# A fused attention and feed-forward kernel on one core: two waits of the last batch's loads exchanged, and two feed-forward tiles of the first stage moved behind scores

## The chip, the cores and the metric

The kernel runs on 1 core of one Trainium2 chip. The metric is the device time of one execution in microseconds (us), as the median of several runs. Engines are named as in the profile: PE (TensorE, matrix products), DVE (VectorE), ACT (ScalarE), POOL (GpSimd), and SP, whose queue issues transfers. POOL also issues transfers, and writes their descriptors itself.

## The reference

Four batches of attention with 8 heads, 768 positions and head size 64 are followed by a feed-forward layer. Each query sees the keys within 15 positions and one summary per block of 32 positions (the maximum of the keys, the mean of the values).

```python
k_sum = k.reshape(B, H, nb, block, D).max(axis=3)
v_sum = v.reshape(B, H, nb, block, D).mean(axis=3)
scores_l = scale * q @ k^T, kept where |i - j| < window, else -1e9
scores_s = scale * einsum('bhsd,bhnd->bhsn', q, k_sum) + log(block)
a = softmax(concat([scores_l, scores_s]))
attn = a @ concat([v, v_sum])
x = attn as [B*S, H*D]                    # 3072 tokens, 512 wide
h = x @ w_in                              # 512 -> 2048
out = (h * sigmoid(1.702 * h)) @ w_out    # 2048 -> 512
```

Inputs and output are float32; the kernel works in bf16 and f16 between them.

## The kernel before, in words

The work is software-pipelined over the four batches: while PE does the feed-forward layer of one batch, the attention of the next is done beside it. A batch's 768 tokens are two halves of 384. The order on each engine is the order in which the program is written: every call goes through `_Ordered`, which keeps it, so an instruction that waits holds up all that stands behind it on its engine. Pools of buffers (`pmm`, four PSUM banks for matmul results; `psb`, two double banks for scores and turned tiles; `outp`, three output tiles `osb`) add waits where a buffer is still in use.

**Batch 0, the lead and the first input stage.** The first half's attention is done by functions of its own up to line 1029. Then the loop of line 1109 does the first feed-forward product of the first half: `ff_in` computes one tile of 128 of the 2048 columns as four matmuls (`ph`) and a GELU activation on ACT into `gT`. There are 16 tiles; two were done earlier (`N0` is 2). `q_late` turns the second half's queries of one head pair with six PE transposes (`ps_q`) and copies them into qT on DVE. The queries of the second half are loaded by POOL into `qb`, head pairs 0 to 3 apart (`load_q1`), between loads of w_in and w_out. Behind the tiles come the scores of the second half (`scores`, one call per head pair, 24 small matmuls `ps_s` and an exponential on ACT), the masks on DVE, the values (`ps_av`) and the turned x (`ps_x`), each put between parts of the first half's output product (`ff_out`, `po`, four matmuls a part) by the table `plan0`. `exp_soon` and `gelu_soon` make ACT load its exponential or GELU table ahead of use.

**Batches 1 to 3.** `load_batch(b)` issues on POOL the four loads of a batch's keys (`kb`, tag kb, two buffers) and the four of its queries (`qb`, two buffers). Transposing transfers on SP turn them: `xk` writes kx from `kb`, `xq` writes qT from `qb`. The values' rows are loaded straight into `vw` (`load_v`), and SP copies parts of them within SBUF (`halo_dmas`). `value_rows` also forms block sums of the values on PE (`ps_vs`), DVE adds them into `vs` (`block_sums`), and SP copies `vs` into `vw` as the sum rows (`sum_dmas`). For batch 3, `load_batch` copies one column to a tile `gate2` on POOL twice, which makes POOL's queue wait there: once for `vs`, once for the turned queries in qT.

In the loop of line 1154 with b = 1, PE does batch 1's feed-forward products: first the input tiles (16 for each half), then the output in seven products for each of three token tiles (`product`, with PSUM tiles poA, poB and poC). The output is put together by DVE in `osb` tiles and stored by SP. Beside it runs batch 2's attention; its result x is turned by transposing transfers on SP (`dx`, into xT). `load_batch(3)` is called after the second product, so that its waits and loads stand on POOL's queue at that place. The loop with b = 2 does the same for batch 2 beside batch 3's attention, with no further batch to load.

Of the kernel before, what the change touches and what calls it, by code (L numbers as in the profile page):

```python
# [9 lines left out]
F32 = mybir.dt.float32  # L10
# [25 lines left out]
def kernel(  # L36
# [10 lines left out]
    B, H, S, D = q.shape  # L47
# [5 lines left out]
    NP = H // 2  # L53
# [5 lines left out]
    NT = d_ff // 128  # L59
    HALF = S // 2  # L60
# [4 lines left out]
    dve = _Ordered(tc, nc.vector)  # L65
    act = _Ordered(tc, nc.scalar)
    pool = _Ordered(tc, nc.gpsimd)
# [55 lines left out]
    def load_turned(x, b, t2, name, gs_=(0, 1)):  # L123

        for g in gs_:
            t2[g] = castp2.tile([128, 2, NJ, 2, D], BF16, name=name, tag=name)
            for hh in range(2):
                h0 = hh * NP + 2 * g
                pool.dma_start(out=t2[g][:, :, :, hh].rearrange("p i a d -> p (i a) d"),
                               in_=x[b, h0:h0 + 2].rearrange("h (a p) d -> p (h a) d", p=128))  # L130

    def load_v(b):
        w5 = vw[b % 2].rearrange("p (j e) h c -> p j e h c", e=2)
        src = v[b].rearrange("h (j e p) d -> e j p h d", e=2, p=64)
        for j in range(NJ):
            for e in range(2):
                pool.dma_start(out=w5[e * 64:e * 64 + 64, j, e, :, 0:D], in_=src[e, j])
# [72 lines left out]
    qTs = [keep.tile([128, NP, S], BF16, name=f"qT{s}") for s in range(2)]  # L210
    qT = [[qTs[s][:, p] for s in range(2)] for p in range(NP)]
    vw = [keep.tile([128, NQ, H, VC], BF16, name=f"vw{s}") for s in range(2)]
    vs = keep.tile([128, H, VC], BF16, name="vs")
# [18 lines left out]
    def clear_values(eng, s):  # L232
        eng.memset(vw[s][96:128, 0], 0.0)
        eng.memset(vw[s][96:128, 0, :, D:VC], 1.0)
        eng.memset(vw[s][32:64, NQ - 1], 0.0)
        eng.memset(vw[s][32:64, NQ - 1, :, D:VC], 1.0)
# [8 lines left out]

    def load_batch(b):
        if b == 3:
            pool.tensor_copy(out=gate2[0:32], in_=vs[0:32, H - 1, 0:1])
        load_turned(k, b, kb2, "kb")
        if b == 3:  # L250
            pool.tensor_copy(out=gate2, in_=qTs[0][:, NP - 1, 0:1])
        load_turned(q, b, qb2, "qb", (0,) if b == 1 else (0, 1))
        if b == 2:
            load_v(b)

    def load_rest1():
        dve.memset(vw[1][:, :, :, D:VC], 1.0)
        clear_values(dve, 1)
        load_v(1)
        load_turned(q, 1, qb2, "qb", (1,))  # L260
# [12 lines left out]
    def copy(eng, out, in_):  # L273
        if eng is act:
            act.activation(out=out, in_=in_, func=ACT.Copy)
        elif eng == "dve_alone":

            dve.tensor_reduce(out=out, in_=in_.unsqueeze(len(in_.shape)), axis=AX.X, op=ALU.max)
        else:
            eng.tensor_copy(out=out, in_=in_)  # L280
# [91 lines left out]
    def turn_plain(ps, src):  # L372

        n, rows = src.shape[0], src.shape[2]
        for r in range(rows):
            for h in range(2):
                pe.transpose(out=ps[h * 64:h * 64 + 64, r * n:r * n + n], in_=src[:, h, r],
                             identity=ident[0:n, 0:n])
# [37 lines left out]
    def q_late(p, eng):  # L416
        if p < 2:
            ps = psb.tile([128, 2048], BF16, name="ps_q", tag="big")
        else:
            ps = pmm.tile([128, 1024], BF16, name="ps_q", tag="mm")  # L420
        turn_plain(ps[:, 0:HALF], qb2["late"][:, 2 * p:2 * p + 2])
        copy(eng, qT[p][0][:, HALF:S].rearrange("p (c r) -> p c r", r=JH),
             ps[:, 0:HALF].rearrange("p (r c) -> p c r", r=JH))
# [164 lines left out]
    def scores(b, half, p):  # L588
        a = a_sb[half, p] = attp.tile([128, 2, TH, QT], BF16, name="a_sb", tag="a_sb")
        big = psb.tile([128, 1024], F32, name="ps_s", tag="big")  # L590
        score_tiles(big, p, b % 2, half)
        act.activation(out=a.rearrange("p h t c -> p h (t c)"),
                       in_=big.rearrange("p (h c) -> p h c", h=2)[:, :, 0:HALF],
                       func=ACT.Exp, scale=scale)

    def mask(half, p):
        a = a_sb[half, p]
        dve.tensor_mul(a, a, mk[:, half * TH:(half + 1) * TH, :].unsqueeze(1)
                       .to_broadcast([128, 2, TH, QT]))

    def values(b, half, g, mm=False, between=()):

        if mm:
            banks = [pmm.tile([128, 512], F32, name="ps_av", tag="mm") for i in range(2)]
        else:
            ps = psb.tile([128, 1024], F32, name="ps_av", tag="big")
            banks = [ps[:, i * 512:i * 512 + 512] for i in range(2)]
        pvs = []
        for i in range(2):
            p = 2 * g + i  # L610
            a = a_sb[half, p]
            pv = banks[i][:, 0:390].rearrange("p (h j c) -> p h j c", h=2, j=JH)
            pvs.append(pv)
            for hh in range(2):
                for j in range(JH):
                    for e in range(2):
                        t = 2 * j + e
                        pe.matmul(out=pv[e * 64:e * 64 + 64, hh, j, :], lhsT=a[:, hh, t, :],
                                  rhs=vw[b % 2][:, half * TH + t, p + hh * NP if b else 2 * p + hh, 0:D + 1],
                                  start=True, stop=True, skip_group_check=True)  # L620
        x2[g] = attp.tile([128, 2, JH, 2, D], F16, name="x2", tag="x2", bufs=4)
        for i in range(2):
            norm(x2[g][:, :, :, i].rearrange("p h j d -> p j h d") if b else x2[g][:, i], pvs[i])
            if i == 0:
                for p in between:
                    mask(half, p)

    def norm(x, pv):
        rc = attp.tile([128, 2, JH, 1], F32, name="rc", tag="rc")
        dve.reciprocal(out=rc, in_=pv[..., D:D + 1])  # L630
        dve.tensor_mul(x.rearrange("p j h d -> p h j d"), pv[..., 0:D],
                       rc.to_broadcast([128, 2, JH, D]))
# [13 lines left out]
    def gelu(half, nt, ph):  # L646
        act.activation(out=gT[half][:, nt, :], in_=ph, func=ACT.Gelu_apprx_sigmoid)
# [3 lines left out]
    def ff_step(ph, half, nt, steps=range(KO)):  # L651
        for n in steps:
            g, i = n // 2, n % 2
            ko = g + 2 * i if halves[0] else 2 * g + i
            pe.matmul(out=ph, lhsT=w_in_sb[:, ko, nt * 128:(nt + 1) * 128],
                      rhs=xTT[half][g][:, i], start=(n == 0), stop=(n == KO - 1))
# [217 lines left out]
    N0 = 2  # L874
# [30 lines left out]
    gate2 = consts.tile([128, 1], BF16, name="gate2")  # L905
# [3 lines left out]
    def gelu_soon():  # L909

        act.activation(out=gate[:, 1:2], in_=gate[:, 0:1], func=ACT.Gelu_apprx_sigmoid)
# [120 lines left out]
    pmm = mid.enter_context(tc.tile_pool(name="pmm", bufs=4, space=bass.MemoryType.PSUM))  # L1032
# [5 lines left out]
    for e in range(2):  # L1038
        r = slice(64 * e, 64 * e + 64)
        dve.tensor_copy(out=w50[r, JH - e:NJ, e, :, 0:D],  # L1040
                        in_=v0n[r, :, JH - e:NJ, 0:D].rearrange("p h j d -> p j h d"))
# [4 lines left out]
    for p in range(NP):  # L1046
        k_late(p, dve)
        key_halos(p, 0, dve, JH)
        key_rows(p, 0, ks0[:, p, 0:nb], dve, JH)
    load_batch(1)  # L1050


    plan0 = {-1: ["s0", "s1"], 0: ["q2"], 1: ["m0", "q3", "m1", "s2", "s3"], 2: ["v0"],
             3: ["v1"], 4: ["x0"]}

    plan1 = {1: ["R"], 2: ["s00", "s01"], 4: ["t2", "t3", "m00", "m01"], 5: ["s10", "s11"],
# [7 lines left out]
    def beside0(slot):  # L1064
        for what in plan0.get(slot, ()):
            i = int(what[1])
            if what[0] == "q":
                q_late(i, dve)
            elif what[0] == "s":
                scores(0, 1, i)  # L1070
                if i == NP - 1:
                    gelu_soon()
            elif what[0] == "m":
                mask(1, i)
            elif what[0] == "v":
                values(0, 1, i, i == 0, (2, 3) if i == 0 else ())
            else:
                tx(1, i, act)

# [26 lines left out]
        sum_dmas(w5, 0)  # L1106


    for nt in range(N0, NT):
        ff_in(0, (nt,))  # L1110
        if nt == 14:
            for p in range(2):
                q_late(p, dve)
    early.close()
# [2 lines left out]
    ws = keep.tile([128, 4, NT // 2, N1], F16, name="ws")  # L1117
    exp_soon()
    beside0(-1)
    load_rest1()  # L1120
    for i, (ms, part) in enumerate((ms, part) for part in range(3) for ms in range(2)):
        ff_out(0, ms, part)
        beside0(i)
    for what, part in ((0, 0), (0, 1), (1, 0), (1, 1), (2, 0), (2, 1), (3, 0), (3, 1)):
        w_sum(what, part)

# [27 lines left out]
    for b in range(1, B - 1):  # L1154
# [34 lines left out]
        i = 0  # L1189
# [101 lines left out]
```

## Time and profile before

| what | value |
|---|---|
| runs | 207.1, 209.39 and 209.02 us; median 209.02 |
| profiled execution, its own time | 208.57 us |
| its span, first to last instruction | 206.6 us |
| PE busy | 196.6 us, 95% of the span |
| DVE busy | 145.3 us, 70% |
| ACT busy | 130.0 us, 63% |
| POOL busy | 91.3 us, 44% |
| loads by POOL's queue | 13.24 MB, 69648 packets |
| transfers by SP's queue | 14.39 MB, 26176 packets |

The profile shows one execution. A row of a timeline gives the start from the beginning of the span, the length, the engine, the line of the program (28 for all instructions, since a helper there records them), the operation with its output and inputs, how many were merged, and in brackets the time for which the engine stood idle before, with what ended it. A landing time is counted from a transfer's issue. In the row of slices the span is cut into 40 parts, and each digit is the busy share of a part in tenths.

### The profile page before, as it was taken

The numbers are of one execution on the slowest core, as the hardware profiler recorded it, in microseconds if no ns is written. First come the engines' busy times: TensorE is split into PE (matmuls) and PEld (weight loads), VectorE is DVE, ScalarE is ACT, GpSimd is POOL, SyncE is SP. The second block draws the span as 40 slices with busy tenths as digits, with TensorE's granted clock in tenths as the row PEclk, the third lists the DMA queues.
The fourth block names the chain that finished last, engine by engine and source line by source line (L and its number), as shares of the span: only waits on it lengthen the run. The fifth ranks groups of instructions, "written<-read, shape, count | busy, mean of one in ns | idle before, by whom it ended". The sixth has DMA issues, their size and how long they took to land.

```text
span 206.6 us, 5962 instructions
## 1 busy us (share of the span) xinstructions
PE 196.6 (95%) x2406; PEld 141.8 (69%) x2406; DVE 145.3 (70%) x397; ACT 130.0 (63%) x250; POOL 91.3 (44%) x141
## 2 busy tenths in 40 slices
PE   6999999999999999999999868999999999999993
PEld 6667654466787876566888744556888865568883
DVE  6676875968787764996769376797867666767221
ACT  4674869378776858778670526778771549985220
POOL 7964589358999521330691006900000008990000
PEclk9999999999999999999999999999999999999999
DMA  6999999999949999997499999999552740000223
GB/s 177 178 170 206 202 224 210 171 153 200 137 67 167 208 185 158 168 135 75 71 174 185 165 159 153 202 138 88 92 155 40 190 132 0 0 0 5 102 105 102
DMA packets 95995, 28.14 MB, mean 136 GB/s; under 512 B 83664, under 2 KB 93152, under 8 KB 95968
## 3 DMA queue, kind: packets, MB, share of 16 engines
q0 software_dynamic: 69648, 13.24, 84.2%
q1 hardware_dynamic: 26176, 14.39, 35.8%
q8 instruction: 19, 0.31, 0.6%
q10 hardware_dynamic: 144, 0.13, 0.2%
q14 instruction: 8, 0.07, 0.1%
HBM read 27.26 MB, written 6.29 MB: 162 GB/s over the span
## 4 chain that ended last, share of the span: by engine, by line
PE 86%; DMA 5%; DVE 4%; ACT 2%; issue 0%; DVEq 0%
PE ph L28 30%; PE poA L28 19%; PE poB L28 9%; PE poC L28 5%; PE phA L28 4%; PE ps_av L28 4%; DMA xT<-x 4%; PE ps_s L28 3%; PE po L28 2%; DVE ks L28 2%; DMA gT<-in_k_dram 2%; PE ps_t L28 1%; PE ps_x L28 1%; DVE qT L28 1%; PE phC L28 1%; PE phB L28 1%
## 5 line engine op out<-in xcount | busy, mean ns | idle before, releaser
L28 PE MATMUL ph<-xT,w_in_sb 128*128 128x384 f16 x400 | 68.1, 326 | 0.9 <-DMA xT<-x 0.8
L28 PEld LDWEIGHTS <-w_in_sb 128*128 128x128 f16 x442 | 42.6, 98 | 28.6 <-issue 1.5
L28 ACT ACTIVATE gT<-ph 128x384 f16<-128x384 f32 x100 | 47.7, 492 | 16.4 <-PE ph L28 15.7
L28 PEld LDWEIGHTS <-gs 128*128 128x128 f16 x352 | 33.5, 98 | 4.3
L28 POOL DMA_DIRECT2D vw<-in_v_dram x36 | 24.6, 700 | 22.2 <-DMA qb<-in_q_dram 13.0
L28 PEld LDWEIGHTS <-gT 128*128 128x128 f16 x296 | 27.8, 98 | 8.7 <-issue 2.7
L28 ACT ACTIVATE a_sb<-ps_s 128x768 bf16<-128x768 f32 (+1 forms) x32 | 24.9, 826 | 7.0 <-PE ps_s L28 6.9
L28 POOL TENSOR_TENSOR gs<-gT 128x384 f16<-128x384 f16 x8 | 7.3, 907 | 36.6 <-ACT gT L28 36.6
L28 DVE TENSOR_TENSOR gs<-gT 128x384 f16<-128x384 f16 (+2 forms) x38 | 16.3, 429 | 9.4 <-ACT gT L28 9.3
L28 PE MATMUL poA<-ws,gs 128*128 128x256 f16 x176 | 22.9, 273 | 0.0
L28 DVE TENSOR_TENSOR x<-ps_av,rc 128x384 f16<-128x384 f32 x32 | 17.8, 558 | 1.1
L28 ACT ACTIVATE osb<-poA 128x256 f32<-128x256 f32 x11 | 4.2, 383 | 19.7 <-PE poA L28 19.7
L28 DVE TENSOR_TENSOR a_sb<-a_sb,mk 128x768 bf16<-128x768 bf16 x28 | 14.4, 553 | 2.8 <-ACT a_sb L28 2.5
L28 POOL DMA_DIRECT2D qb<-in_q_dram x16 | 15.1, 966 | 3.0 <-DMA v0n<-in_v_dram 1.8
L28 ACT ACTIVATE s<-poA 128x256 f32<-128x256 f32 x17 | 6.5, 385 | 12.7 <-PE poA L28 12.7
L28 PEld LDWEIGHTS <-kx 64*128 64x128 bf16 (+1 forms) x378 | 9.9, 95 | 6.3 <-issue 2.5
L28 PE MATMUL poA<-ws,gT 128*128 128x256 f16 x88 | 11.4, 273 | 2.5 <-DVE osb L28 2.5
L28 POOL DMA_DIRECT2D kb<-in_k_dram x14 | 13.6, 990 | 0.0
L28 DVE TENSOR_REDUCE ks<-kx 128x24 bf16<-128x768 bf16 x12 | 11.4, 948 | 3.1 <-ACT kx L28 3.1
L28 ACT ACT_TABLE_LOAD x10 | 12.8, 1283 | 1.0 <-PEq L1275 0.8
L28 PE MATMUL poB<-ws,gs 128*128 128x256 f16 x88 | 11.4, 273 | 0.1
L28 PE MATMUL poA<-w_out_sb,gT 128*128 128x256 f16 x88 | 11.5, 273 | 0.0
(117 smaller groups left out, 296.7 us busy)
## 6 DMA issues: line engine op xcount, KB each, us to landing
out_dram<-osb SPq DMA_DIRECT2D x22, 256.0 KB, 5.3
kb<-in_k_dram POOLq DMA_DIRECT2D x14, 192.0 KB, 7.8
qb<-in_q_dram POOLq DMA_DIRECT2D x12, 192.0 KB, 11.9
vw<-in_v_dram POOLq DMA_DIRECT2D x36, 64.0 KB, 7.7
w_out_sb<-in_moe_w_out_dram POOLq DMA_DIRECT2D x4, 512.0 KB, 13.3
w_in_sb<-in_moe_w_in_dram POOLq DMA_DIRECT2D x3, 512.0 KB, 12.4
vw<-vs SPq DMA_DIRECT2D x6, 198.0 KB, 3.6
gT<-in_k_dram SPq DMA_DIRECT2D x2, 384.0 KB, 3.5
```

The lines of the kernel that those rows point to most:

```text
L28: r = f(*a, **kw)
```

## The change

In `load_batch` the two copies into `gate2` change places: the one from qT now stands ahead of the key loads, the one from `vs` ahead of the query loads. In the first input stage the loop ends two tiles earlier, tiles 14 and 15 are computed behind scores 0 and 1 of the second half, with the query turns 2 and 3 between them, and their GELU activations come after scores 3. The query turns 0 and 1 stand two tiles earlier. In `plan0` the entries of the query turns go, and the first values take a `psb` tile instead of two `pmm` banks.

```diff
     def load_batch(b):
         if b == 3:
-            pool.tensor_copy(out=gate2[0:32], in_=vs[0:32, H - 1, 0:1])
+            pool.tensor_copy(out=gate2, in_=qTs[0][:, NP - 1, 0:1])
         load_turned(k, b, kb2, "kb")
         if b == 3:
-            pool.tensor_copy(out=gate2, in_=qTs[0][:, NP - 1, 0:1])
+            pool.tensor_copy(out=gate2[0:32], in_=vs[0:32, H - 1, 0:1])
         load_turned(q, b, qb2, "qb", (0,) if b == 1 else (0, 1))
...
-    plan0 = {-1: ["s0", "s1"], 0: ["q2"], 1: ["m0", "q3", "m1", "s2", "s3"], 2: ["v0"],
+    plan0 = {-1: ["s0", "s1"], 1: ["m0", "m1", "s2", "s3"], 2: ["v0"],
              3: ["v1"], 4: ["x0"]}
...
-                values(0, 1, i, i == 0, (2, 3) if i == 0 else ())
+                values(0, 1, i, False, (2, 3) if i == 0 else ())
...
-    for nt in range(N0, NT):
+    for nt in range(N0, NT - 2):
         ff_in(0, (nt,))
-        if nt == 14:
+        if nt == 12:
             for p in range(2):
                 q_late(p, dve)
...
     beside0(-1)
     load_rest1()
+    held = []
+    for nt in range(NT - 2, NT):
+        held.append(pmm.tile([128, HALF], F32, name="ph", tag="mm"))
+        ff_step(held[-1], 0, nt)
+        if len(held) == 1:
+            q_late(2, dve)
+            q_late(3, dve)
     for i, (ms, part) in enumerate((ms, part) for part in range(3) for ms in range(2)):
         ff_out(0, ms, part)
         beside0(i)
+        if i == 1:
+            for nt, ph in zip(range(NT - 2, NT), held):
+                gelu(0, nt, ph)
```

On POOL, where batch 3's loads stand (`gate` is the copy into `gate2`, the first number the partitions):

```order
 L28 DMA vw_92<-in_v_dram 64x8x64 x12
+L28 COPY gate_106<-qT_90 128x1
+L28 DMA kb<-in_k_dram 128x12x64 x4
 L28 COPY gate_106<-vs 32x1
-L28 DMA kb<-in_k_dram 128x12x64 x4
-L28 COPY gate_106<-qT_90 128x1
 L28 DMA qb<-in_q_dram 128x12x64 x4
```

The key loads moved ahead of the copy that waits for `vs`; the query loads still stand behind both copies.

On PE, at the end of the first input stage, in the kernel before (the first row of each group; `ph` is a feed-forward tile, numbered by order of use, `ps_q` a query turn, `ps_s` scores, `po` an output part):

```order
L28 MATMUL ps_q_757<-wide_80,qb_134 64x128
...
L28 MATMUL ph_765<-xT00_98,w_in_sb_103 128x384
...
L28 MATMUL ps_s_779<-qT0_90,kx0_88 128x64
...
L28 MATMUL ps_s_794<-qT0_90,kx0_88 128x64
...
L28 MATMUL po_828<-w_out_sb_104,gT_102 128x512
...
L28 MATMUL ps_q_833<-wide_80,qb_134 64x128
...
L28 MATMUL po_841<-w_out_sb_104,gT_102 128x512
...
L28 MATMUL ps_q_847<-wide_80,qb_134 64x128
...
L28 MATMUL ps_s_857<-qT0_90,kx0_88 128x64
```

And the same place of the changed kernel, from the second query turn on:

```order
L28 MATMUL ps_q_745<-wide_80,qb_134 64x128
...
L28 MATMUL ph_753<-xT00_98,w_in_sb_103 128x384
...
L28 MATMUL ps_s_767<-qT0_90,kx0_88 128x64
...
L28 MATMUL ps_s_782<-qT0_90,kx0_88 128x64
...
L28 MATMUL ph_816<-xT00_98,w_in_sb_103 128x384
...
L28 MATMUL ps_q_821<-wide_80,qb_134 64x128
...
L28 MATMUL ps_q_829<-wide_80,qb_134 64x128
...
L28 MATMUL ph_837<-xT00_98,w_in_sb_103 128x384
...
L28 MATMUL po_842<-w_out_sb_104,gT_102 128x512
...
L28 MATMUL po_847<-w_out_sb_104,gT_102 128x512
...
L28 MATMUL ps_s_855<-qT0_90,kx0_88 128x64
```

Query turns 2 and 3 (833 and 847 before, 821 and 829 now) moved from between the output parts to between the last two tiles, and those tiles to behind scores 1.

On DVE at the same place (`qT` the query copies, `a_sb` the masks, `rc` the first norm of the values):

```order
 L28 MEMSET vw_93 32x8x2
-L28 COPY qT_90<-ps_q 128x384
-L28 TENSOR_TENSOR a_sb<-a_sb,mk 128x768
-L28 COPY qT_90<-ps_q 128x384
-L28 TENSOR_TENSOR a_sb<-a_sb,mk 128x768
```

```order
+L28 COPY qT_90<-ps_q 128x384 x2
+L28 TENSOR_TENSOR a_sb<-a_sb,mk 128x768 x2
+L28 RECIPROCAL rc<-ps_av 128x6
+L28 TENSOR_TENSOR x_916<-ps_av,rc 128x2x3x64
+L28 TENSOR_TENSOR a_sb<-a_sb,mk 128x768 x2
```

The two query copies, which stood before and between the masks, now stand together ahead of both.

## The prediction

> **What bounds the kernel now.** I read the busy shares in slices first, then who TensorE (PE) waits for, then the timelines of the engines at each of those waits, and last the landing times of the transfers there. The slice row of the DMA engines and PE's largest waits after the lead-in:
>
> ```profile
> DMA  6999999999949999997499999999552740000223
> PE poA L28 <- DVE osb L28: 2.5, 1, 2.5
> PE ph L28 <- DMA xT<-x: 0.8, 1, 0.8
> ```
>
> PE's waits are few, and only they can be won. These two are the largest of the main program; they lie at 118 to 125 us, in batch 1's product stage and just behind it (a third, of 0.5 us at 34 us, is shown further down). There the timelines of PE, VectorE (DVE) and the sync queue (SP) read (start, length, what; the idle time before in brackets):
>
> ```profile
> 120.49 1.03 PE L28 MATMUL poA<-ws,gT 128*128 128x256 f16 x8 [2.48 <-DVE osb L28]
> 121.36 3.12 PE L28 MATMUL ph<-xT,w_in_sb 128*128 128x384 f16 x18
> 125.29 18.04 PE L28 MATMUL ph<-xT,w_in_sb 128*128 128x384 f16 x110 [0.81 <-DMA xT<-x]
> 120.02 0.42 DVE L28 TENSOR_TENSOR osb<-poA,s 128x256 f32<-128x256 f32 x1 [3.23 <-DMA out_dram<-osb]
> 112.29 0.34 SPq L28 DMA_DIRECT2D out_dram<-osb  x1
> 114.79 5.40 SPq L28 DMA_TRANSPOSE xT<-x  x2
> ```
>
> The last product of tile 2 waits for DVE, which waits from 116.79 for an output tile: there are three `osb` buffers, and the third was still being stored. That store was issued at 112.29. PE's next wait is for the last turned x of batch 2, whose transposes were issued from 114.79. Both waits are late transfers. How late is seen by comparing the same transfers in this stage (first two rows, the store alone and the four transposes) and in batch 2's stage at 156 to 164 us (last two), where no loads run:
>
> ```profile
> out_dram<-osb SPq DMA_DIRECT2D x1, 256.0 KB, 7.6
> xT<-x SPq DMA_TRANSPOSE x4, 8.1
> out_dram<-osb SPq DMA_DIRECT2D x2, 256.0 KB, 2.3
> xT<-x SPq DMA_TRANSPOSE x4, 2.8
> ```
>
> A store takes 7.6 us instead of 2.3, a transpose 8.1 instead of 2.8, and PE has no such wait in the later stage. What differs is batch 3's eight loads, seen on GpSimd's queue (POOL), with the DMA share (the next to last number, in which the queues are added, so that it can pass 1) before and during them:
>
> ```profile
> 100.15 0.57 POOL L28 COPY gate<-vs 32x1 bf16<-32x1 bf16 x1 [10.19 <-DVE vs L28]
> 100.66 4.06 POOL L28 DMA_DIRECT2D kb<-in_k_dram  x4
> 105.10 4.04 POOL L28 DMA_DIRECT2D qb<-in_q_dram  x4
> 94.00:104.00 10.00, 10.00 (x188) 7.75 (x186) 7.43 (x21) 7.50 (x13) 3.85 (x5) 1.00 0.50 79
> 104.00:120.00 16.00, 14.01 (x226) 11.98 (x224) 9.21 (x25) 6.28 (x13) 5.14 (x6) 1.00 1.98 176
> ```
>
> The loads stand for 10.19 us behind the block sums while the DMA engines are half idle, and then fill them until after the stores and transposes.
>
> **The batch 3 loads.** The copy into `gate2` from qT and the one from vs change places, so the k loads wait only for the turned queries of batch 2, and the q loads for the block sums. When the turned queries are there, and how long the loads take (the last rows are the first k load and the last two q loads, with shortest, median and longest landing):
>
> ```profile
> L28 SPq DMA_TRANSPOSE qT<-qb x2: 1837/3424/5012, 76.9 to 84.5; - x2
> qT<-qb SPq DMA_TRANSPOSE x1, 8.5
> kb<-in_k_dram POOLq DMA_DIRECT2D x1, 192.0 KB, 5.8
> L28 POOL DMA_DIRECT2D qb<-in_q_dram x2: 1037/1042/1047, 107.1 to 108.1; - x2
> DMA to landing us min/median/max: 12.7/14.3/16.0
> ```
>
> The second transpose, issued at 84.5, takes 8.5 us: qT is there at 93.0. With the copy's 0.57 us the first k load goes at about 93.6 instead of 100.66, 7.1 us earlier; the four issues then end at 97.7. The copy from vs starts at 100.15 as now, and the q loads go at about 100.7, 4.4 us earlier. Before, the first load lands at 100.66 + 5.8 = 106.5 and the last at 108.1 + 16.0 = 124.1: seven loads in 17.6 us, 2.5 us each. After, the first lands at 99.4, the last at that pace at 117.0. That pace was held beside two stores and four transposes, so 117 is the late end. The early end is the last q load's issue, 100.7 + 3 x 1.01 = 103.7, with the 5.8 us of an unhindered load: 109.5. I take 114, nearer to the late end because the row of the slow pace is these same loads. So the DMA engines are free of loads from about 114, not from 124.
>
> The store of 112.29 has to land by 116.8 less a signal's time, 0.13 (112.29 + 7.6 = 119.89, and DVE goes on at 120.02): it may take 4.4 us. With the loads gone at 114 it lands near 115.5, and nothing is left of the 2.48 us; gone at 117, it lands near 117.8 and 1.0 us is left. The transposes issued from 114.79 are then the next to be late: the second goes by 117.5 (half of 5.40 later), takes 2.8 us and lands near 120.3, while PE, with its 2.48 us won, wants it at 125.29 - 0.81 - 2.48 = 122.0; so the 0.81 us goes too. From here to the end PE shows no further wait of this kind, so what is won stays won. **Gain: 3.29 us less 0 to 1.0; I take 3.0.** Ends of the range: 3.3, and 0.5 if the store still lands in 7 us.
>
> What the early loads can harm is what SP moves from 94 to 104 us, above all the copies of the block-sum rows, which the values of batch 2 read. The rows: their issue, their landing, the landing of the same copies of batch 1 (at 59.7 us, under loads just issued), and the first reader:
>
> ```profile
> 100.11 1.24 SPq L28 DMA_DIRECT2D vw<-vs  x2
> vw<-vs SPq DMA_DIRECT2D x2, 198.0 KB, 3.4
> vw<-vs SPq DMA_DIRECT2D x2, 198.0 KB, 5.4
> 108.11 0.95 PE L28 MATMUL ps_av<-vw,a_sb 128*64 128x65 bf16 x48
> ```
>
> The second copy goes at about 100.7 and may take 108.11 - 0.13 - 100.7 = 7.3 us. At 5.4 it costs nothing; at the 7.6 of the slowed store 0.3 us; at three times its 3.4 us, as store and transposes grew (7.6 to 2.3, 8.1 to 2.8), 10.2 and so 2.9 us. The nearest row is the one of the same copy, so I take 0, and keep 0 to 2.9.
>
> The Trainium skill bears on this (DMA: Bandwidth & Descriptors, section "Queues, rings and completion order"): each DMA engine takes turns between the queues that have work, a packet at a time. By that rule a copy from SP is slowed as soon as loads are pending, however many there are, to about half speed: twice 3.4, an estimate of 6.8 us for the sum rows, under the limit. It speaks against the change in one way: a backlog that is shorter but not over slows a store as much as a long one. The rows of the slowed store and transposes, near three times and not two, go further than the rule.
>
> **The first input stage.** Instead of tiles 2 to 15 in one go, PE does 2 to 12, the first two query turns, tile 13, scores 0 and 1, tile 14, query turns 2 and 3, tile 15, and then the output parts. No matmul is added or taken away. Queries 2 and 3 are turned, and so needed, earlier. PE's rows of before, DVE's copies, the two loads on POOL with their landing (shortest, median, longest), and of ScalarE (ACT) the exponentials, the next work behind them, and the groups of table loads and GELU activations:
>
> ```profile
> 19.87 9.59 PE L28 MATMUL ph<-xT,w_in_sb 128*128 128x384 f16 x58
> 32.47 1.04 PE L28 MATMUL po<-w_out_sb,gT 128*128 128x512 f16 x4
> 33.44 0.36 PE L28 MATMUL ps_q<-wide,qb 128*64 128x128 bf16 x6
> 33.73 0.35 PE L28 MATMUL ps_s<-qT,kx 64*128 64x64 bf16 x12
> 34.59 0.35 PE L28 MATMUL ps_s<-qT,kx 64*128 64x64 bf16 x12 [0.51 <-DVE qT L28]
> 29.85 1.02 DVE L28 COPY qT<-ps_q 128x384 bf16<-128x384 bf16 x2 [1.13 <-PE ps_q L28]
> 17.22 0.70 POOL L28 DMA_DIRECT2D qb<-in_q_dram  x1 [0.61 <-DMA w_in_sb<-in_moe_w_in_dram]
> 18.54 0.71 POOL L28 DMA_DIRECT2D qb<-in_q_dram  x1 [0.62 <-DMA w_in_sb<-in_moe_w_in_dram]
> DMA to landing us min/median/max: 13.2/13.6/13.9
> 32.62 3.19 ACT L28 ACTIVATE a_sb<-ps_s 128x768 bf16<-128x768 f32 x4
> 39.76 0.81 ACT L28 ACTIVATE xT<-ps_x 128x768 f16<-128x768 f16 x1 [2.44 <-PE ps_x L28]
> L28 ACT ACT_TABLE_LOAD x10 | 12.8, 1283 | 1.0 <-PEq L1275 0.8
> L28 ACT ACTIVATE gT<-ph 128x384 f16<-128x384 f32 x100 | 47.7, 492 | 16.4 <-PE ph L28 15.7
> ```
>
> One tile of four matmuls is 9.59 / 58 x 4 = 0.66 us. The run of tiles ends two tiles earlier, at 29.46 - 1.32 = 28.1; with two query turns of 0.29 (33.44 to 33.73) tile 13 ends near 29.3. DVE was idle 1.13 us before its copies, so it can begin them at 28.7; the second is done at 29.7, scores 1 end near 30.0 and tile 14 near 30.7. Now PE wants query 2, which by the order of issue (13.9, then 13.2 us) landed at 31.1, and query 3, at 31.7. **Before, PE took them at 32.2 and 33.4, when they were long there; now it stands for them.** Query 3's turns start at 31.74 + 0.13 = 31.87. Then come these 0.29, tile 15 with 0.66, two output parts with 0.97 each (32.47 to 33.44) and scores 2 and 3 with about 0.28 each: 35.3. Before, scores 3 were through at 34.87 by the same measure (34.59 + 0.28). The wait of 0.51 us goes, since DVE now copies queries 2 and 3 before the masks and not between them, but about 1.0 us of waiting for the loads takes its place. **Cost: 0.45 us.** Its ends: -0.5, if the loads land 0.7 us earlier and only the 0.51 goes; +1.2, if they land 0.7 later.
>
> The two GELU activations go behind the second table load on ACT. The exponentials take 0.80 each (3.19 / 4): with scores 2 through at 35.0, the last ends near 36.7, and the table load and two activations (1.28 and 0.49 each) near 39.0, ahead of ACT's next work at 39.8; I cost them at nothing. That gap of 2.44 us is the cover; beyond it PE's next input stage would come later one for one. The values of the first pair move to the other PSUM pool, where they wait for the exponential of scores 2, over near 35.9, while PE gets there near 36.3, behind one more output part: nothing either.
>
> **The sum**, made on the profiled execution: 208.57 + 0.45 - 3.0 = 206.0. That execution is 0.45 below the median of the runs shown, 209.02, so I predict **206.2**.
>
> **The rivals.** First, *the backlog is thinner but not over*: loads that still run at 112 to 117 slow the store as they do now, which would be so if they keep 2.5 us each and the sum-row copies and stores push them on. Then the store lands near 118 to 119, 1 to 2 us of the first wait stay, and the time is 207.0 to 208.5. For it speaks that the last q load is still issued at 103.7; against it the half-idle 10 us that the k loads now use. The Trainium skill's rule on turns, from the page and section named above, would bring this about.
>
> Second, *the early part gains as well*: if queries 2 and 3 land before 30.7, the term is -0.5 and the time 205.2. The landing rows speak against it, since nothing ahead of those loads on their queue changes.
>
> Third, on the slower side, *the sum rows come late*: one unbroken run of loads from 94 us on slows the copies of 100.11 as the transposes of qT were at their worst. The row of 8.5 us gives 1.2 us of waiting at 108.11; it decides from 7.3 us of landing on. Were they as slow as the q loads themselves, 12.7 us, values wait 5.4 us: 208.57 + 0.45 + 5.4 - 3.0 = 211.4. The same copy's 5.4 us at 59.7 speaks against it.
>
> Fourth, *the change doesn't do what it says*: the k loads wait for something else. Only their buffers could hold them, and those were emptied by the key transposes before the query ones. The time would be 209.0 with the early cost.
>
> **How the numbers follow.** Forecast (205.4 to 206.9) 0.51; thinner backlog 0.24; early gain too 0.10; sum rows late 0.09; no earlier loads 0.06. The range leaves out the late sum rows, the loads that don't move and a little at each end, 0.17 in all: 204.9 to 208.5. About 1%, 2.1 us, is what a measurement of this kernel can tell from no change. Faster by more than 1% (below 206.9) are the forecast and the early gain, 0.61; slower by more than 1% (above 211.1) is the worse part of the late sum rows, 0.06; within 1% is the rest, 0.33.
>
> **What would show it.** In the changed profile the k loads start near 94 and the q loads near 101; the store ahead of tile 2's end lands in under 5 us; PE's wait for `osb` is under 1 us and the one for `xT` is gone. At 31 us PE waits for `qb` twice, about 1 us in all, and no longer for DVE's qT before scores 3. PE's values of batch 2 start without a wait. The prediction is wrong if the store still takes 7 us, if PE stops ahead of the values at 108 us, or if the early part loses more than 1.2 us.

## The result, and the profile after

The changed kernel's median is 207.49 us (20 runs, 205.33 to 209.29) beside 209.07 us (20 runs) of the kernel before on the same chip. The ratio is 0.9903 with an interval of 0.9873 to 0.9932: 2.0 us faster (1.4 to 2.7), at the edge of what can be told from no change. The sign was forecast, and the time lies in the range of 204.9 to 208.5; but it is outside the band of 205.4 to 206.9 to which the forecast itself gave its chance of 0.51, and the gain is smaller than the 2.8 us between the two medians of the prediction. A ratio leaves out slow executions and a median does not, so a ratio need not be the quotient of two medians.

The profiled execution of the changed kernel takes 205.86 us, its span is 203.8 us. First the page: the DMA engines' row of slices, and the chain that ended last. Then all waits of PE that the view of waits lists (total, times, longest):

```profile
DMA  6999999999979999999999979999242830000223
PE 93%; DVE 3%; DMA 2%; ACT 1%; issue 0%; DVEq 0%
```

```profile
PE ps_h L28 <- DVE warm L28: 1.3, 1, 1.3
PE ps_k L28 <- ACT kb L28: 0.5, 1, 0.5
PE ps_b L28 <- DVE ks L28: 0.4, 1, 0.4
PE ps_av L28 <- DVE a_sb L28: 0.4, 1, 0.4
```

Both waits on which the prediction rested, for `osb` and for `xT`, are off the list; what is left belongs to the lead and to the first values. In the slice row the digits 7 and 4 of before, at 93 to 103 us, are now 9 and 9; what was half idle there is used. The timelines around the two places, in the order of the prediction (start, length, work, idle time before):

```profile
93.15 0.19 POOL L28 COPY gate<-qT 128x1 bf16<-128x1 bf16 x1 [2.04 <-DMA qT<-qb]
93.66 4.05 POOL L28 DMA_DIRECT2D kb<-in_k_dram  x4 [0.32 <-issue]
101.14 0.50 POOL L28 COPY gate<-vs 32x1 bf16<-32x1 bf16 x1 [3.42 <-DVE vs L28]
101.65 4.04 POOL L28 DMA_DIRECT2D qb<-in_q_dram  x4
...
101.03 1.24 SPq L28 DMA_DIRECT2D vw<-vs  x2
...
109.03 0.95 PE L28 MATMUL ps_av<-vw,a_sb 128*64 128x65 bf16 x48
...
118.16 0.42 DVE L28 TENSOR_TENSOR osb<-poA,s 128x256 f32<-128x256 f32 x1 [0.45 <-PE poA L28]
...
118.77 1.04 PE L28 MATMUL poA<-ws,gT 128*128 128x256 f16 x8
119.64 6.66 PE L28 MATMUL ph<-xT,w_in_sb 128*128 128x384 f16 x40
```

The k loads go at 93.66, the q loads at 101.65. DVE waits 0.45 us for PE where it waited 3.23 us for a store, and PE runs through. The landings of the transfers of SP between 112 and 118 us (mean size, median landing), and the last row those of the sum rows issued at 101:

```profile
out_dram<-osb SPq DMA_DIRECT2D x2, 256.0 KB, 2.9
xT<-x SPq DMA_TRANSPOSE x4, 3.1
...
vw<-vs SPq DMA_DIRECT2D x2, 198.0 KB, 4.9
```

The store fell from 7.6 us to 2.9 (the median of two) and the transposes from 8.1 to 3.1, close to the 2.3 and 2.8 of the undisturbed stage. The sum rows grew from 3.4 to 4.9 us, within the 7.3 that they had, and the values start at 109.03 without a wait. The first input stage, on PE:

```profile
29.27 0.53 PE L28 MATMUL ps_q<-wide,qb 128*64 128x128 bf16 x12
29.73 0.82 PE L28 MATMUL ph<-xT,w_in_sb 128*128 128x384 f16 x4
30.68 0.82 PE L28 MATMUL ps_s<-qT,kx 64*128 64x64 bf16 x24
31.43 0.82 PE L28 MATMUL ph<-xT,w_in_sb 128*128 128x384 f16 x4
32.18 0.53 PE L28 MATMUL ps_q<-wide,qb 128*64 128x128 bf16 x12
32.64 0.82 PE L28 MATMUL ph<-xT,w_in_sb 128*128 128x384 f16 x4
33.30 1.89 PE L28 MATMUL po<-w_out_sb,gT 128*128 128x512 f16 x8
35.12 0.53 PE L28 MATMUL ps_s<-qT,kx 64*128 64x64 bf16 x24
35.58 1.04 PE L28 MATMUL po<-w_out_sb,gT 128*128 128x512 f16 x4
```

Here the waits for `qb` that were foretold are missing, because everything came about 1.2 us later: the query turns start at 29.27, not at 28.1. From their start to the output part behind scores 3 this takes 35.58 - 29.27 = 6.31 us. Before, counting from a start two tiles earlier (29.39 - 1.30 = 28.09) to the part at 34.87, it was 6.78.

So the two profiled executions differ by three things. The lead, whose instructions are the same, is 1.19 us slower (the first tile of the stage at 20.40 instead of 19.21). Some 0.3 of that is won back by 117 us. The rest is the waits: the input product behind tile 2 starts at 119.64 instead of 121.36, batch 3's first scores at 140.54 instead of 143.25, and the span is 2.8 us shorter. Without the slower lead this one pair would show nearly 4 us, about twice what the 20 runs show. The question is where the other executions give it back.

### The profile page after: what moved, and what is told of

It reads as the page before. It is cut to its first block, busy times and chain, and to the rows that moved or that the text cites. A ratio compares the mean times of both kernels' runs of the same rounds, so it can differ in the third digit from the quotient of the medians.

```text
span 203.8 us, 5963 instructions
## 1 busy us (share of the span) xinstructions
PE 197.7 (97%) x2406; PEld 143.0 (70%) x2406; DVE 145.3 (71%) x397; ACT 129.6 (64%) x250; POOL 92.3 (45%) x141
## 3 DMA queue, kind: packets, MB, share of 16 engines
q1 hardware_dynamic: 26176, 14.39, 35.2%
## 4 chain that ended last, share of the span: by engine, by line
PE 93%; DVE 3%; DMA 2%; ACT 1%; issue 0%; DVEq 0%
PE ph L28 32%; PE poA L28 20%; PE poB L28 10%; PE poC L28 5%; PE phA L28 4%; PE ps_av L28 4%; PE ps_s L28 4%; PE po L28 3%; DMA gT<-in_k_dram 2%; PE ps_t L28 1%; PE ps_x L28 1%; PE ps_k L28 1%; PE phC L28 1%; PE phB L28 1%; PE phE L28 1%; DVE qT L28 1%
## 5 line engine op out<-in xcount | busy, mean ns | idle before, releaser
L28 POOL DMA_DIRECT2D vw<-in_v_dram x36 | 25.4, 722 | 23.0 <-DMA qb<-in_q_dram 14.5
L28 PE MATMUL poB<-w_out_sb,gs 128*128 128x256 f16 x88 | 11.4, 273 | 0.0
```

The lines of the kernel that those rows point to most:

```text
L28: r = f(*a, **kw)
```

## The experiments

Ratios are to the kernel before on the same chip, with their intervals. The runs of one table row were made beside those of the same group.

| group | kernel | median us | ratio | interval |
|---|---|---|---|---|
| 1 (before 209.40) | exchange of the waits alone | 207.62 | 0.987 | 0.9818 to 0.9922 |
| 1 | first stage alone | 209.81 | 1.0009 | 0.997 to 1.0047 |
| 1 | changed kernel | 207.64 | 0.9877 | 0.9819 to 0.9935 |
| 1 | k and q loads wait for qT only | 207.28 | 0.989 | 0.9851 to 0.9929 |
| 2 (before 210.01) | before, k loads without a wait | 206.61 | 0.9824 | 0.9785 to 0.9864 |
| 2 | changed, k loads without a wait | 206.45 | 0.9823 | 0.9782 to 0.9864 |
| 2 | changed, batch 0's queries earlier | 207.29 | 0.9853 | 0.9808 to 0.9897 |
| 2 | changed, both (k loads without a wait, queries earlier) | 206.18 | 0.9806 | 0.9763 to 0.985 |
| 3 (before 209.76) | changed kernel | 207.45 | 0.9882 | 0.9831 to 0.9934 |
| 3 | changed, k loads without a wait | 206.12 | 0.9825 | 0.9771 to 0.988 |
| 3 | changed, both | 205.62 | 0.9799 | 0.9747 to 0.985 |
| 3 | changed, both, longer warm-up | 205.96 | 0.9806 | 0.9747 to 0.9864 |

**The halves of the change.** The theory: the exchange of the two waits brings all of the gain, and the first stage costs a little or nothing. The rival: the first stage wins as well. The exchange alone is the hunk in `load_batch`; its counterpart is all the rest of the diff.

```diff
-            pool.tensor_copy(out=gate2[0:32], in_=vs[0:32, H - 1, 0:1])
+            pool.tensor_copy(out=gate2, in_=qTs[0][:, NP - 1, 0:1])
         load_turned(k, b, kb2, "kb")
         if b == 3:
-            pool.tensor_copy(out=gate2, in_=qTs[0][:, NP - 1, 0:1])
+            pool.tensor_copy(out=gate2[0:32], in_=vs[0:32, H - 1, 0:1])
```

Expected of the exchange alone:

> The exchange of the two waits alone; the first input stage is as before. Theory (the loads' backlog makes the two waits of 3.3 us at 118 to 125 us, and the exchange takes them away; the first stage is worth about nothing on average): 3.0 us less, ratio 0.986, and the profile has no PE wait for osb or xT. Rival (the exchange is worth only what the whole change measured, 2 us or less, because some of the wait stays in most executions): ratio 0.990 to 0.993, and part of the wait for osb is seen.

Expected of the first stage alone:

> The first input stage's change alone; batch 3's loads wait as before. Theory (query turns 2 and 3 now come when their loads land, so an execution whose lead is quick stands about 1 us for them, and one whose lead is slow gains 0.5 us): between 0.5 us less and 0.5 us more, ratio 0.998 to 1.002, and in the profile PE's end of scores 3 is never before 35.2 us, whenever the turns begin. Rival (it gains its 0.5 us or more by itself): ratio 0.997 or below.

Expected of the changed kernel beside them:

> The changed kernel again. Theory: ratio 0.990 as measured; in the profile the load waits at 31 us are seen if PE's first turns come before 28.6 us and not if they come after, while the part from 97 us on reads as in its first profile, with no wait for osb or xT. Rival (the first profile was a lucky one): a wait for osb of 1 us or more is back in this one.

By the ratios, the exchange alone saves 2.7 us (1.6 to 3.8), the first stage alone costs 0.2 (from a gain of 0.6 to a cost of 1.0), and the whole, 2.6 us (1.4 to 3.8), is about their sum. By the medians of this group the exchange and the whole save 1.8 us each, which the intervals hold as well; so their size is known to about a microsecond, their equality better. With the first stage alone both waits stay, and those for the queries foretold at 31 us appear. PE's largest waits of that kernel, then PE's rows of its first stage:

```profile
PE poA L28 <- DVE osb L28: 1.9, 1, 1.9
PE ph L28 <- DMA xT<-x: 1.8, 1, 1.8
```

```profile
28.28 0.53 PE L28 MATMUL ps_q<-wide,qb 128*64 128x128 bf16 x12
...
31.40 0.36 PE L28 MATMUL ps_q<-wide,qb 128*64 128x128 bf16 x6 [0.31 <-DMA qb<-in_q_dram]
32.09 0.36 PE L28 MATMUL ps_q<-wide,qb 128*64 128x128 bf16 x6 [0.33 <-DMA qb<-in_q_dram]
...
35.32 1.04 PE L28 MATMUL po<-w_out_sb,gT 128*128 128x512 f16 x4
```

Turns at 28.28, output part at 35.32: 7.04 us, 0.26 more than before. The two stalls of batch 1's stage add up to 3.7 us here, not to the 3.29 of the profile from which I predicted: the exchange had more to win than I counted.

But with the exchange alone, and again in this second profile of the changed kernel, something stands in the list of waits that the first profile did not have. From the exchange alone, PE's waits and the two rows in which they lie, then POOL's rows, then the landing of batch 2's sum rows:

```profile
PE ps_av L28 <- DMA vw<-vs: 1.2, 2, 0.8
...
68.63 0.54 PE L28 MATMUL ps_av<-vw,a_sb 128*64 128x65 bf16 x23 [0.76 <-DMA vw<-vs]
...
110.84 0.92 PE L28 MATMUL ps_av<-vw,a_sb 128*64 128x65 bf16 x47 [0.47 <-DMA vw<-vs]
```

```profile
95.72 0.22 POOL L28 COPY gate<-qT 128x1 bf16<-128x1 bf16 x1 [6.62 <-DMA qT<-qb]
96.23 4.05 POOL L28 DMA_DIRECT2D kb<-in_k_dram  x4 [0.29 <-issue]
```

```profile
vw<-vs SPq DMA_DIRECT2D x2, 198.0 KB, 8.4
```

The turned queries of batch 2 are there at 95.7, 2.6 us later than in the profile of the changed kernel, so the k loads start later, and the sum rows copied at 101.61 land in 8.4 us instead of 4.9: PE stands 0.47 us ahead of batch 2's values. The other 0.76 us, at 68.63, is for batch 1's sum rows, some 27 us ahead of the loads that were moved, and so not the exchange's doing. The second profile of the changed kernel has the stop at batch 2's values longer:

```profile
109.98 0.19 PE L28 MATMUL ps_av<-vw,a_sb 128*64 128x65 bf16 x1 [0.72 <-DMA vw<-vs]
111.15 0.92 PE L28 MATMUL ps_av<-vw,a_sb 128*64 128x65 bf16 x47 [0.98 <-DMA vw<-vs]
```

That is the prediction's third rival, in part of the executions.

**What makes the sum rows late.** Two theories. One: the q loads that start with the sum rows slow them, so that without the wait for `vs` ahead of the q loads they would be later still. The other: the k loads are still unfinished when the sum rows go, so that what counts is how far ahead of the sum rows they start. The first kernel drops the wait for `vs`, so that q follows k at once:

```diff
-            pool.tensor_copy(out=gate2[0:32], in_=vs[0:32, H - 1, 0:1])
-        load_turned(k, b, kb2, "kb")
-        if b == 3:
             pool.tensor_copy(out=gate2, in_=qTs[0][:, NP - 1, 0:1])
+        load_turned(k, b, kb2, "kb")
```

> Batch 3's k and q loads both wait for the turned queries alone, and none for the block sums; the first stage as before. Theory: the q loads go at 98 instead of 101 us; the sum-row copies land in 5 to 7 us, under the 7.3 they may take, and the waits at 118 to 125 are gone as with the exchange, so the time is that of the exchange alone within 0.3%. Rival (sum rows late): PE waits 1 us or more ahead of batch 2's values, and the time is 0.5% or more above the exchange alone.

The next two leave the k loads no wait but that for their own buffers, and put q behind `vs`; one on the kernel before, one on the changed one:

```diff
-        if b == 3:
-            pool.tensor_copy(out=gate2[0:32], in_=vs[0:32, H - 1, 0:1])
         load_turned(k, b, kb2, "kb")
         if b == 3:
-            pool.tensor_copy(out=gate2, in_=qTs[0][:, NP - 1, 0:1])
+            pool.tensor_copy(out=gate2[0:32], in_=vs[0:32, H - 1, 0:1])
```

> The exchange without the wait for the turned queries: batch 3's k loads wait for nothing but their buffers, its q loads for the block sums; the first stage as before. Theory (in the exchange the k loads, begun at 94 to 97 us, are still running when the sum-row copies go at 101 us, and PE stood 1.2 to 1.7 us ahead of batch 2's values in two of three profiles): the k loads go at 90 us and land by 101, the sum-row copies land in under 7 us, the wait ahead of the values is gone and the two at 118 to 125 us too; 1 us less than the exchange alone, ratio 0.981 to 0.984. Rival (the k loads now slow the turning of batch 2's queries, so scores or halo copies come late): a PE wait ahead of scores at 96 to 106 us, ratio 0.987 or above.

> The changed kernel without the wait for the turned queries (first stage as changed). Theory: as the k loads without a wait on the kernel before, within 0.2%, since the first stage's change measured 1.001; ratio 0.981 to 0.985. Rival: the first stage's change loses 0.5 us or more here, ratio 0.986 or above.

(The 1.2 us that the first of these texts names for the exchange is the sum of both rows above; 0.47 of it is batch 2's.)

Without the wait for `vs` (k at 95.99, q at 100.00) PE stands 2.1 us ahead of the values, the longest of all. The rival's wait came, but not its time: the ratio is 0.989 beside the exchange's 0.987, within the 0.3% of the theory. This is the row:

```profile
110.31 0.92 PE L28 MATMUL ps_av<-vw,a_sb 128*64 128x65 bf16 x47 [2.05 <-DMA vw<-vs]
```

With the k loads set free on the kernel before, they start at 92.08, and the wait is gone. POOL's rows, and the landing of the sum rows:

```profile
92.08 4.32 POOL L28 DMA_DIRECT2D kb<-in_k_dram  x4
100.40 0.57 POOL L28 COPY gate<-vs 32x1 bf16<-32x1 bf16 x1 [4.00 <-DVE vs L28]
```

```profile
vw<-vs SPq DMA_DIRECT2D x2, 198.0 KB, 6.4
```

That kernel gains 3.7 us (2.9 to 4.5), by the ratios a microsecond more than the exchange, though on another chip. Put side by side, the profiles of all kernels that move the k loads fall into two groups (the start is that of the first k load; in the last three rows one or more of the others followed 1.7 to 4.1 us behind it):

| kernel | k loads start | sum rows issued | k ahead by | sum rows land in | PE's wait ahead of batch 2's values |
|---|---|---|---|---|---|
| second profile of the changed kernel | 97.77 | 101.19 | 3.4 | 8.9 | 1.7 |
| changed, batch 0's queries earlier | 95.86 | 99.66 | 3.8 | 8.3 | 1.1 |
| both wait for qT only | 95.99 | 99.99 | 4.0 | 8.8 | 2.1 |
| exchange alone | 96.23 | 101.61 | 5.4 | 8.4 | 0.5 |
| changed, first profile | 93.66 | 101.03 | 7.4 | 4.9 | none |
| changed, both | 93.19 | 100.83 | 7.6 | 7.0 | none |
| changed, third profile | 94.32 | 102.16 | 7.8 | 5.6 | none |
| changed, both, repeated | 92.33 | 100.37 | 8.0 | 6.0 | none |
| before, k loads free | 92.08 | 100.36 | 8.3 | 6.4 | none |
| changed, both, longer warm-up | 92.45 | 101.10 | 8.7 | 7.1 | 0.2 |
| changed, k loads free | 90.81 | 101.97 | 11.2 | 5.4 | none |
| the same, repeated | 89.79 | 102.23 | 12.4 | 4.7 | none |

With a head start (the column "k ahead by") of 7.4 us or more the sum rows land in 7.1 us or less, and PE waits 0.2 us at most; with 5.4 or less they take 8.3 to 8.9, and PE waits 0.5 to 2.1. This speaks for the second theory, since the q loads start within about a microsecond of the sum rows' issue in all of them. In the kernel before, the first of eight loads starts 0.55 us behind the sum rows, and these land in 3.4 us; loads that start beside them are thus not enough to make them late. Counted from its issue with the longest landing of the four, the last k load is out until 7 to 12 us behind the sum rows' issue in the first four rows of the table, and until 1 to 5 us behind it in the others. The first theory keeps a share: the kernel without the wait for `vs` has the longest stop, although its head start isn't the shortest.

A third theory would be that late turned queries and late sum rows are two signs of one crowded moment, without the k loads as the cause. The free k loads speak against it: on the kernel before, the second query transpose goes at 84.16 and takes at least 11.3 us, so the queries are there at 95.5 at the earliest, about as late as with the exchange alone (95.72), and yet the sum rows land in 6.4 us.

In the kernels that still wait for qT the head start is a matter of when the turned queries arrive, anything from 93.15 to 97.25 us.

**The first stage with earlier queries.** If the loads of queries 2 and 3 set the cost of the first stage, loading them ahead of the first piece of w_out removes it:

```diff
-    for a in range(2):
+    for a in range(NP):
         load_q1(a)
     load_w_out(0)
-    for a in range(2, NP):
-        load_q1(a)
```

> The changed kernel with the loads of queries 2 and 3 of batch 0 ahead of the first load of w_out on POOL's queue. Theory (the moved query turns wait for these loads, 0.64 us in the first stage's own profile): the loads land 1 to 3 us earlier, PE has no wait for qb, and the time is 0.3 to 0.6 us below the changed kernel, ratio 0.985. Rival (another wait takes its place, for DVE's query copies or for w_out, which now lands 1 us later): ratio 0.988 as the changed kernel, and a wait for w_out or qT at 30 to 36 us.

> The changed kernel with both edits: k loads of batch 3 without a wait, and queries 2 and 3 of batch 0 loaded ahead of w_out. Theory: the two gains add up, 1.3 to 1.6 us below the changed kernel, ratio 0.979 to 0.982. Rival: neither helps, ratio 0.987 to 0.989.

The wait for `qb` goes. On PE in the first of the two:

```profile
27.96 0.53 PE L28 MATMUL ps_q<-wide,qb 128*64 128x128 bf16 x12
...
34.29 1.04 PE L28 MATMUL po<-w_out_sb,gT 128*128 128x512 f16 x4
```

6.33 us from turns to output part, where the changed kernel takes 6.80 when its turns start as early (third profile, of group 3: 28.10 to 34.90, with a wait of 0.44). In these two profiles the gain is about half a microsecond. The times agree in sign (a ratio of 0.9853 where the changed kernel has 0.9877 to 0.9903; with the k loads free 206.18 us against 206.45), but the intervals overlap. The same kernel's profile also shows the sum rows late (1.1 us) and the wait for `osb` still at 1.3 us: its store landed in 6.1 us. The prediction's first rival, a thinner backlog, thus happens too, in one of the six profiles whose k loads wait for qT.

**The versions beside each other on one chip.** Does freeing the k loads help the changed kernel, and does a longer warm-up of PE steady the lead? The last kernel has `idle(31)` for `idle(28)`, three more warm-up matmuls; the other three are as above.

> The changed kernel once more, beside the next three on one chip. Theory (its gain of 3.3 us at 118 to 125 us is partly given back ahead of batch 2's values, by how late the turned queries of batch 2 start the k loads): ratio 0.987 to 0.990; if the k loads start at 95 us or later the profile has a wait for the sum rows of 1 us or more, if they start at 94 or earlier it has none.

> The changed kernel without the k loads' wait for the turned queries, again. Theory (the wait for the sum rows is what the changed kernel gives back): 1 to 1.5 us below the changed kernel on the same chip, ratio 0.981 to 0.984, no PE wait for sum rows. Rival (the difference between chips made it): within 0.4 us of the changed kernel.

> The changed kernel with free k loads and with queries 2 and 3 of batch 0 loaded ahead of w_out, again. Theory: 0.2 to 0.4 us below the one with free k loads alone, since the waits for qb of up to 0.64 us go and one for the first part of w_out of up to 0.4 us comes in their place; ratio 0.979 to 0.982. Rival: no different from it, within 0.1 us.

> As the one before, with 31 instead of 28 idle matmuls ahead of the first key turn (they compute nothing that is used), so that PE does not stand for 0.2 to 0.5 us between them and the first keys. Theory (PE runs its first microseconds at half pace and gets quick at 6 to 11 us in different executions; a gap in its work can put that off): PE is quick by 7 us and the time is 0 to 0.3 us lower with fewer late ones. Rival (the moment does not hang on that gap): same time, and the profile may show the slow pace past 7 us all the same.

On the same chip the changed kernel takes 207.45 us, with the k loads free 206.12, with early queries as well 205.62. This last is the best of all: 2% under the kernel before (0.9747 to 0.985) and, by the medians, 1.8 us under the changed one. Its profile shows no wait of PE for a load, a store or the sum rows at all:

```profile
PE ps_h L28 <- DVE warm L28: 1.3, 1, 1.3
PE ps_k L28 <- ACT kb L28: 0.9, 2, 0.4
PE ps_b L28 <- DVE ks L28: 0.8, 2, 0.4
PE ps_av L28 <- DVE a_sb L28: 0.4, 1, 0.4
PE ps_vt L28 <- issue: 0.2, 1, 0.2
```

With the k loads free but the queries at their old place, PE's wait for `qb` is in this group's profile the largest seen, 0.96 and 0.28 us, and the first stage takes 35.49 - 28.00 = 7.49 us; the profile of the same kernel in group 2 has 0.32 us and 6.79. The longer warm-up brought nothing (205.96 us, and matmuls at full pace from 7.1 us on as in others): inconclusive at best.

One row stays unexplained. The changed kernel's third profile, the one of group 3, has a gap of 1.7 us ahead of part of batch 1's values at 73.9 us, and one with free k loads has 1.5 us at 73.7. The profile names no releaser, and this lies ahead of batch 3's loads, as the exchange's 0.76 us at 68.63 does; so it isn't the work of the edits to those loads:

```profile
73.90 0.44 PE L28 MATMUL ps_av<-vw,a_sb 128*64 128x65 bf16 x15 [1.69 <-issue]
```

Are PE's waits the whole of what differs? Take each of the fourteen spans, and subtract the start of the stage's first tile (19.1 to 20.4 us) and all idle times of PE behind it that its timeline lists: what is left is 183.0 to 183.6 us in every one. So, to within 0.6 us, the executions differ by their lead and by PE's listed waits. Behind the lead these waits are 4.0 and 4.7 us in the two kernels with the old order, 0.4 to 2.8 (mean 2.2) in the six profiles whose k loads wait for qT, and 0.4 to 2.6 (mean 1.5) in the six with free k loads.

## Why the prediction was right, and where it was not

- **What bounds: right.** The two waits at 118 to 125 us came from late transfers behind the backlog of batch 3's loads. With the loads moved and nothing else, store and transposes land in 4.2 and 4.6 us and both waits are gone; with everything but the loads changed, they take 7.8 and 8.1 and the waits are there.
- **When the loads go: right in one profile, taken as fixed in all.** 93.6 was foretold and 93.66 came; the last q load was through by 113.7 at the latest (issued by 104.6, at most 9.1 us to land), against 114. But the 93.0 at which the turned queries arrive came from one execution. In the five other profiles where the k loads wait for them, the copy behind them starts at 93.80 to 97.25.
- **Gain 3.0: too small.** This term of the sum was sized from one execution with 3.29 us of waits, and 0.3 was taken off. Another profile with those loads in place shows 3.7 us, and the kernel in which nothing is given back, the free k loads on the kernel before, gains 3.7 (2.9 to 4.5).
- **Sum rows at no cost: the step that failed.** I took the nearest row, 5.4 us of landing, and gave a late landing a chance of 0.09. Four of the six profiles whose k loads wait for the turned queries show PE stopped ahead of batch 2's values, by 0.5, 1.7, 2.1 and 1.1 us, a mean of 0.9 over the six. This is one of the signs by which the prediction called itself wrong, and it is about the third rival's price (1.2 us from an 8.5 us landing) at a chance some seven times as high. The first profile, which agrees with every sign from 93 us on, was a lucky draw. That the other kernels, without that wait, are 1.0 (exchange and free k loads on the kernel before, in two groups) to 1.3 us faster (changed kernel, one chip) fits it; that all of this difference lies at the sum rows isn't shown, since the changed kernel's third profile has no such wait and the timed runs have no profile.
- **First stage +0.45: right in mechanism, its size hangs on the lead.** When the loads land doesn't follow the lead: where PE had to wait, it went on with query 3's turns at 31.66 to 32.26 us, against the 31.87 of the prediction, while its own arrival moves with the lead. With turns starting at 28.0 to 28.3 the stage takes 6.79 to 7.49 us, with turns at 29.27 it takes 6.31 and 6.36 and there is no wait; before it was 6.78. That spread, +0.7 to -0.5, lies within the ends that I gave, and the mean effect is 0.2 us (-0.6 to +1.0). The wait of DVE's qT at 34 us is gone, as foretold. I had expected of the first stage alone that scores 3 never end before 35.2 us; in two later profiles of that stage the output part behind them starts at 34.9.
- **GELUs and values pool at nothing: nearly.** PE's wait ahead of the second values of the first pair grew from 0.2 to 0.4 us. The GELUs end at 39.3, ACT's next work is at 40.65.
- **From the sum to the median.** The sum gave 206.0 for an execution of 208.57; carried to the median of 209.02, that is 206.45. I wrote 206.2 and so added 0.25 us of gain that no step holds.

Against a gain of 2.55 us by the sum, three comparisons measured 2.0, 2.6 and 2.5 us by the ratios (1.6, 1.8 and 2.3 by the medians). That is close, but in part by luck, since two misses offset each other: the waits were worth more than 3.0, and by the profiles about 0.9 was given back at the sum rows.

The Trainium skill's rule on turns (DMA: Bandwidth & Descriptors, section "Queues, rings and completion order") has each DMA engine go round the queues that have work, a packet at a time. The estimate that the prediction made from it, half pace as soon as loads are pending, was 6.8 us for the sum rows; they took 4.9 to 8.9, on both sides of it, and what told them apart was how far the loads had come. The rule names the sharing; that dependence it does not give.

## What to carry to other kernels

A wait that holds back a batch of loads has two sides: too late, and the backlog slows what comes behind; moved only part of the way, and it slows a smaller transfer that somebody wants at once. Ask how far ahead of that transfer the loads start, and prefer a place with a margin wider than the event varies: here the k loads needed none of the waits that they were given, and without them they started at 89.8 to 93.2 us, not steadier than the 93.7 to 97.8 behind the wait, but early enough in every profile. And when a load is to start by an event at the end of a busy queue, one profile gives one draw of it; look at that event in several executions before a margin of a few microseconds is called safe.

## What the runs showed of the hardware

The lead, the same instructions in every kernel up to 13 us but for three warm-up matmuls in one, runs at two paces, and the moment at which it turns to the faster one is not fixed. Twelve turns of `ps_k` take 0.85 us at the slow pace and 0.53 at the fast one. In the profile of before:

```profile
4.96 0.85 PE L28 MATMUL ps_k<-wide,kb 128*64 128x128 bf16 x12 [0.49 <-ACT kb L28]
...
6.62 0.53 PE L28 MATMUL ps_k<-wide,kb 128*64 128x128 bf16 x12
```

and of the changed kernel:

```profile
7.08 0.85 PE L28 MATMUL ps_k<-wide,kb 128*64 128x128 bf16 x12
...
11.05 0.53 PE L28 MATMUL ps_k<-wide,kb 128*64 128x128 bf16 x12
```

The fast pace begins at about 5 us in three profiles (0.53 or 0.54 us from 4.91, 4.92 and 5.04 on), at about 6 to 7 us in most, and between 10.3 and 11.05 us in the first of the changed kernel, which accounts for its 1.19 us of late start. The granted clock in the row of slices reads 9 (90% or more) all through. The Trainium skill (TensorE: Matmul & The Clock Gate, "Part 1: The HAM clock gate") has matmuls at half rate until a free-running window of about 3.4 us has been busy, and a turn that varies by about half a microsecond. The two paces and a moving turn agree with it: four more `ps_h` matmuls take 0.43 us at the slow pace (1.06 for eight, 0.63 for four) and 0.22 at the fast one (0.61 and 0.39). A turn past 10.3 us, about 9 us after the first matmul at 1.30, is later than that. The length of the short gap near 4.5 us doesn't decide it alone: gaps of 0.43 to 0.57 us stand ahead of the turns at 5 us, gaps of 0.19 to 0.50 ahead of the later ones.

The same copy of batch 2's 198 KB within the chip took from 3.4 to 8.9 us, by what loads were still being served, and the same 256 KB store from 2.3 us with no loads beside it to 7.8 us. Such a landing time describes what else was on its way, not the transfer.
